# Two decode layers on one core: a 22nd cache unit kept on chip between the layers, four slots left for what is loaded there

## The chip, the cores and the metric

The kernel runs on one core of a Trainium2 chip. The metric is device time in microseconds (us), the median of three runs; lower is better. Beside it stands one profiled execution, whose trace gives the durations used below.

## The reference

The same pair of blocks is applied twice to a row `x` of 448 numbers for each of 2 batch entries (B = 2, D = 448): an attention block over a cache, and a gated feed-forward block (called FFN below). All data is float32.

```python
def _A_ref(x, k_cache, v_cache, wq, wo):        # H = 16 heads, Dh = 256, Sk = 4096
    q = (x @ wq) ... one query of 256 per head and batch entry
    scores = einsum("bhqd,bhkd->bhqk", q, k_cache) * Dh ** -0.5
    p = softmax(scores)
    o = einsum("bhqk,bhkd->bhqd", p, v_cache)
    return o ... @ wo
def _B_ref(x, W_gate, W_up, W_down):             # F = 1792
    gate = relu(x @ W_gate); up = x @ W_up
    return (gate * up) @ W_down

x = x + _A_ref(_layernorm(x), k_cache, v_cache, wq, wo)
x = x + _B_ref(_layernorm(x), W_gate, W_up, W_down)
x = x + _A_ref(_layernorm(x), k_cache, v_cache, wq, wo)      # same weights, same cache
x = x + _B_ref(_layernorm(x), W_gate, W_up, W_down)
```

The cache has 32 pairs of a head and a batch entry. Keys and values of one pair are 4 MB each, so one attention block reads 256 MB and the whole kernel a little over twice that.

## The kernel before

**Slots and units.** All loaded data goes through one on-chip tile, `arena`, cut into 27 slots of 128 partitions by 2048 numbers (1 MB): 24 slots in three blocks of eight, and three single slots. A quarter of one pair's keys or values fills one slot and is called a unit here: `("k", pair, c)` or `("v", pair, c)` with c from 0 to 3. The weights of one head (query and output projection, `("h", head, 0)`), one of seven parts of `W_gate` and `W_up` (`("in", "", c)`, here in 0 to in 6) and one of four parts of `W_down` (`("out", "", c)`, here out 0 to out 3) also take one slot each, with 128x1792 numbers or less (896 KB). Units go into the 24 block slots alone, a head's weights into the three single slots alone, and FFN weights into a single slot first and otherwise into any.

**The list of loads.** `pending` is a list of all loads in a fixed order: those of the first attention (pass 1), the eleven FFN loads, those of the second attention (pass 2), the eleven FFN loads again. `pump()` (L115) takes loads from its front as long as a slot of the right kind is free and issues each as a DMA from SyncE (SP in the profile); when the first in the list finds no slot, nothing behind it goes. It is called whenever `release()` (L144) frees a slot, that is, behind the last instruction that reads the slot. So each DMA waits on SP for the reader whose release made it possible, and the DMAs keep the order of the list.

**What is kept over the turn.** The turn is the end of pass 1, the FFN, and the start of pass 2. Pass 2 goes through the pairs in the order `second`, which begins with the last four pairs of pass 1. Units in the set `keep` (L186) are not released by pass 1, stay in their slots over the FFN, and are left out of the loads of pass 2. Before the change `keep` has the weights of the first head, the first 20 units of pass 2 (keys of pairs 0, 1 and 2, values of pairs 0 and 1, four each) and the last quarter of the values of pair 2: 21 units and one head, 22 slots. Five slots are left for the FFN's eleven loads, two of them single slots. As `keep` takes the loads for granted, pass 2 loads first, in this order: three quarters of the keys of pair 3, the weights of two heads (`heads`, placed by L192), the last quarter of those keys, three quarters of the values of pair 2, and then whole sets of four.

**The work at the turn.** The FFN (`ffn`, L560) first makes the layer's input row ready (`absorb`), then multiplies it with in 0 to in 3 (L576, 32 matmuls), with in 3 again and in 4 (16 matmuls), in 5 (8) and in 6 (8), with other matmuls of TensorE (PE) in between, then with out 0 to out 3 (L669). Each part is released behind its last matmul. Pass 2 starts with the scores of pair 0 on VectorE and ScalarE (`score`, L393 on): a kept unit is released behind its score. The query of pair 2 (`query`, L326) is made in the first iteration of pass 2, between scores, and needs the first of the two heads.

**In the steady part** of a pass, `score_block` (L370) works on the keys of one pair with two long VectorE instructions (L378 and L386), and `weigh` (L453) multiplies the values on TensorE. Several megabytes of loads are in the DMA queue at any time there.

Of the kernel before, what the change touches and what calls it, by code (L numbers as in the profile page):

```python
# [21 lines left out]
NC = NT // CT  # L22
# [48 lines left out]
def two_layers(  # L71
# [77 lines left out]
    second = first[-1:-5:-1] + first[:-4]  # L149
    behind = dict(zip(first[1:], first))  # L150

    def loads(order, whole, cuts):


        found = [(("h", order[0][0], 0), 1)]

        def some(kind, u):
            c = 0
            for n in cuts.get((kind, u), (NC,)):
                found.append(((kind, order[u], c), n))  # L160
                c += n

        for u, unit in enumerate(order):
            if u in whole:
                found.append((("k", unit, 0), PAIR))
            else:
                some("k", u)
                if u > 0:
                    some("v", u - 1)
            if u % 2 and u + 1 < len(order):  # L170
                found.append((("h", order[u + 1][0], 0), 1))
        some("v", len(order) - 1)
        return found
# [10 lines left out]
    of_second = loads(second, WHOLE_SECOND, early | at_end)  # L184

    keep = {of_second[0][0], *[key for key, _ in of_second if key[0] != "h"][:KEPT]}  # L186
    keep.add(("v", second[2], NC - 1))
    of_second = [(key, n) for key, n in of_second if key not in keep]

    heads = [(key, n) for key, n in of_second if key[0] == "h"][:2]  # L190
    of_second = [part for part in of_second if part not in heads]
    of_second[NC - 1 : NC - 1] = heads  # L192
    pending += of_first + [(key, 1) for key in ffn_loads]
    pending += of_second + [(key, 1) for key in ffn_loads]

# [617 lines left out]
def build(nc, shapes):  # L813
    import concourse.tile as _tile

    args = [
        nc.dram_tensor(f"in_{n}_dram", s, F32, kind="ExternalInput").ap() for n, s in shapes.items()
    ]
    for i, (shape, _) in enumerate(_OUTS):
        args.append(nc.dram_tensor(f"out_{i}_dram", shape, F32, kind="ExternalOutput").ap())  # L820
    with _tile.TileContext(nc) as tc:
        two_layers(tc, *args)
# [12 lines left out]
```

## Time and profile before

| | before |
|---|---|
| median of 3 runs | 1320.49 us (1320.46 to 1320.8) |
| the profiled execution's own time | 1320.27 us |
| its span, first to last instruction | 1318.5 us |
| moved by DMA in the span | 563.16 MB, mean 427 GB/s |
| busy: VectorE / TensorE / GpSimd / ScalarE | 82% / 42% / 20% / 15% |
| granted TensorE clock, mean | 0.682 |

The time outside the span is 1.8 us. All times in the trace are counted from the start of the span. In the tables of stretches that the prediction shows, "DMA share" is the mean busy share of the core's 16 DMA engines; a little over 1.00 stands for full, since packets of one engine overlap slightly in the records. A line of the DMA issues gives size and the time from issue to landing, where the profile can tell it.

### The profile page before, as it was taken

The page shows a single profiled execution, that of the slowest core. Times are in us where ns is not written, and L with a number is a line of the kernel's source. Part 1 is how long each engine was busy: PE and PEld are TensorE (multiplying, and loading weights), DVE is VectorE, ACT ScalarE, POOL GpSimd, SP SyncE. Part 2 cuts the span into 40 slices and gives each one's busy share as a digit, 9 for nine tenths or more (in the row PEclk, how much of TensorE's full clock was granted, in tenths as well). Part 3 has the DMA queues.
Part 4 walks back from the last instruction along what each step waited for, and adds up shares of the span by engine and source line. Part 5 has one row for each costly group of instructions (what it writes and reads, how often), then busy time and mean ns, then how long its engine had stood idle before and what let it go on. Part 6 is the DMA issues. An engine that isn't in the chain of part 4 may idle for free.

```text
span 1318.5 us, 9085 instructions
## 1 busy us (share of the span) xinstructions
PE 553.7 (42%) x3276; PEld 190.6 (14%) x3276; DVE 1081.6 (82%) x780; ACT 195.6 (15%) x776; POOL 269.0 (20%) x192
## 2 busy tenths in 40 slices
PE   2243342433434324345585444242433424434348
PEld 2011010110111101112141111110111101101113
DVE  4989888898888988888729987798888988877892
ACT  2100000000000000212026513000000000012241
POOL 0002003322133220321001153030123331230210
PEclk9675666656667667666697777666767667666679
DMA  9999999999999999999999999999999999999998
GB/s 408 435 430 429 432 428 437 432 436 434 417 445 435 430 430 426 445 418 430 421 405 416 431 430 435 438 432 430 432 431 436 433 428 436 429 432 425 427 425 334
DMA packets 22665, 563.16 MB, mean 427 GB/s; under 512 B 2520, under 2 KB 2652, under 8 KB 9564
## 3 DMA queue, kind: packets, MB, share of 16 engines
q1 hardware_dynamic: 22612, 562.57, 99.5%
q8 instruction: 26, 0.43, 0.1%
q14 instruction: 19, 0.16, 0.0%
q10 hardware_dynamic: 8, 0.00, 0.0%
HBM read 562.56 MB, written 0.00 MB: 427 GB/s over the span
## 4 chain that ended last, share of the span: by engine, by line
DMA 55%; DVE 32%; PE 7%; POOL 2%; issue 2%; ACT 1%; DVEq 0%; SPq 0%; POOLq 0%; ACTq 0%
DMA arena<-in_vk_dram 54%; DVE arena L378 12%; DVE scores L386 11%; DVE arena L409 3%; DVE down L418 2%; PE po L462 2%; POOL top L429 2%; DVE arena L418 2%; DMA arena<-in_w_out_dram 1%; DVE row L478 1%; PE small L488 1%; PE acc L511 1%; DVE scores L415 1%; ACT arena L411 1%; PE pf L576 1%
## 5 line engine op out<-in xcount | busy, mean ns | idle before, releaser
L378 DVE TENSOR_TENSOR arena<-arena 128x8192 f32<-128x8192 f32 x51 | 443.3, 8692 | 111.0 <-DMA arena<-in_vk_dram 110.9
L386 DVE TENSOR_REDUCE scores<-arena 128x32 f32<-128x8192 f32 (+1 forms) x53 | 431.8, 8148 | 0.0
L488 PE MATMUL small<-ones,row 128*128 128x1 f32 x256 | 62.0, 346 | 686.3 <-DVE row L478 686.3
L462 PE MATMUL po<-arena,probs 128*2 128x512 f32 x2048 | 303.1, 734 | 10.3 <-DMA arena<-in_vk_dram 6.6
L429 POOL PARTITION_ALL_REDUCE top<-mx x64 | 64.6, 1009 | 645.8 <-DVE mx L427 645.8
L443 POOL PARTITION_ALL_REDUCE total<-rs x64 | 176.1, 2752 | 61.3 <-ACT probs L437 60.3
L488 PEld LDWEIGHTS small<-ones,row 128*128 128x128 f32 x256 | 56.5, 308 | 748.9 <-DVE row L478 748.9
L434 ACT ACTIVATE nm<-top,nsr 128x1 f32<-128x1 f32 x64 | 18.8, 294 | 612.4 <-POOL top L429 612.4
L354 POOL PARTITION_BROADCAST arena<-arena x58 | 27.6, 545 | 300.6 <-ACT arena L350 300.6
L462 PEld LDWEIGHTS po<-arena,probs 128*2 128x2 f32 x2048 | 54.8, 96 | 198.3 <-issue 191.2
L338 PE MATMUL pq<-arena,xs 128*33 128x256 f32 x174 | 70.6, 571 | 14.1 <-DMA arena<-in_w_head_dram 14.1
L511 PE MATMUL acc<-arena,oT 128*2 128x448 f32 x128 | 50.9, 894 | 32.1 <-DVE oT L501 32.1
L350 ACT ACTIVATE arena<-pq 33x256 f32<-33x256 f32 x29 | 10.9, 377 | 321.7 <-PE pq L342 321.7
L382 ACT ACTIVATE arena<-arena 128x256 f32<-128x256 f32 x104 | 41.7, 402 | 86.2 <-DVE arena L378 86.2
L478 DVE SCALAR_TENSOR_TENSOR row<-po,lead,row 128x256 f32<-128x256 f32 x64 | 30.7, 479 | 25.8 <-ACT row L475 25.4
L411 ACT ACTIVATE arena<-arena 128x256 f32<-128x256 f32 x117 | 47.1, 404 | 20.4 <-DVE arena L409 20.1
L409 DVE TENSOR_TENSOR arena<-arena 128x1024 f32<-128x1024 f32 (+1 forms) x24 | 42.0, 1748 | 0.0
L338 PEld LDWEIGHTS pq<-arena,xs 128*33 128x33 f32 x174 | 25.3, 162 | 81.3 <-issue 66.7
L475 ACT ACTIVATE row<-po,lead 128x256 f32<-128x256 f32 x64 | 29.1, 455 | 21.2 <-PE po L462 21.2
L418 DVE SCALAR_TENSOR_TENSOR down<-arena,pq 128x256 f32<-128x256 f32 x64 | 26.9, 420 | 5.4 <-DMA arena<-in_vk_dram 3.4
L501 DVE TENSOR_TENSOR oT<-small,ri 128x4 f32<-128x4 f32 x32 | 5.1, 161 | 29.0 <-PE small L488 29.0
L437 ACT ACTIVATE probs<-scores,nm,sr 128x32 f32<-128x32 f32 x64 | 26.4, 413 | 2.1
(145 smaller groups left out, 359.0 us busy)
## 6 DMA issues: line engine op xcount, KB each, us to landing
arena<-in_vk_dram SPq DMA_DIRECT2D x16, 4096.0 KB, 40.0
arena<-in_w_head_dram SPq DMA_DIRECT2D x31, 896.0 KB, 30.9
arena<-in_vk_dram SPq DMA_DIRECT2D x27, 1024.0 KB, 14.9
arena<-in_vk_dram SPq DMA_DIRECT2D x12, 2048.0 KB, 38.5
arena<-in_w_in_dram SPq DMA_DIRECT2D x14, 896.0 KB, 26.2
arena<-in_w_out_dram SPq DMA_DIRECT2D x5, 896.0 KB, 8.9
arena<-in_vk_dram SPq DMA_DIRECT2D x47, 43.4
arena<-in_w_out_dram SPq DMA_DIRECT2D x1, 512.0 KB, 17.3
```

Of the source, the lines that this page charges most:

```text
L338: nc.tensor.matmul(q, xs[:, c, :], w[:, c * DH : (c + 1) * DH], start=(c == 0), stop=False)
L378: nc.vector.tensor_mul(kt, kt, q_of[u][:, None, :].to_broadcast([P, NT, DH]))
L386: nc.vector.reduce_sum(s_of[u][:, shared:], kt[:, shared:, :], axis=AX.X)
L409: nc.vector.tensor_mul(some, some, q_of[u][:, None, :].to_broadcast([P, whole, DH]))
L411: nc.scalar.activation(kt[:, t, :], kt[:, t, :], AF.Copy, accum_out=found[:, t : t + 1])
L418: nc.vector.scalar_tensor_tensor(junk if kept else kt[:, t, :], kt[:, t, :], 1.0, q_of[u], op0=ALU.mult, op1=ALU.mult, accum_out=found[:, ...
L429: nc.gpsimd.partition_all_reduce(mx_of[u], mx, P, RED.max)
L443: nc.gpsimd.partition_all_reduce(total[:, b : b + 1], rs, P, RED.add)
L462: nc.tensor.matmul(po_of[u][32 * t : 32 * t + 2, :], p_of[u][:, n : n + 2], vt[:, 2 * t * DH : (2 * t + 2) * DH], start=(c == 0), stop=(c ...
L478: nc.vector.scalar_tensor_tensor(row[:, :DH], po_of.pop(u)[:, DH:], lead[:, 1:2], row[:, :DH], op0=ALU.mult, op1=ALU.add,)
L488: nc.tensor.matmul(pT_of[u - u % 2][:, c, b : b + 1], row[:, c * P : (c + 1) * P], ones, start=True, stop=True,)
L511: nc.tensor.matmul(acc[at : at + B], oT_of[h][:, c, :], wo[:, c * D : (c + 1) * D], start=(n < 3), stop=(n >= n_u - 3),)
```

## The change

One more unit is kept: the third quarter of the values of pair 2 in the order of pass 2 stays in its slot, beside the fourth. With 22 units and one head, 23 of the 27 slots are taken over the FFN and four are free, two of them single. One load of 1 MB leaves the list of pass 2. In that list the weights of the two heads now come first, ahead of all keys of pair 3, where three units stood ahead of them before.

```diff
     keep = {of_second[0][0], *[key for key, _ in of_second if key[0] != "h"][:KEPT]}
-    keep.add(("v", second[2], NC - 1))
+    keep |= {("v", second[2], c) for c in (NC - 2, NC - 1)}
     of_second = [(key, n) for key, n in of_second if key not in keep]
 
     heads = [(key, n) for key, n in of_second if key[0] == "h"][:2]
     of_second = [part for part in of_second if part not in heads]
-    of_second[NC - 1 : NC - 1] = heads
+    of_second[:0] = heads
```

The instructions of TensorE, VectorE, ScalarE and GpSimd stand in the same order as before. On SP one DMA is gone and two have moved. The first piece below is SP's queue between the FFN of the turn and the start of pass 2, with - for before and + for after (`in_vk_dram` holds keys and values, 128x2048 is one unit, `in_w_head_dram` the weights of a head, `in_w_out_dram` those of `W_down`):

```order
 L131 DMA arena<-in_w_out_dram 128x1792 x3
 L131 DMA arena<-in_w_out_dram 128x896
-L131 DMA arena<-in_vk_dram 128x2048 x3
 L131 DMA arena<-in_w_head_dram 128x1792 x2
-L131 DMA arena<-in_vk_dram 128x2048 x20
+L131 DMA arena<-in_vk_dram 128x2048 x22
 L131 DMA arena<-in_w_head_dram 128x1792
 L131 DMA arena<-in_vk_dram 128x8192 x4
```

The two heads have moved ahead of three units, and 23 single units have become 22; everything behind is as it was. What this piece does not show is for which reader each DMA waits. The second piece is SP's queue over the FFN's own loads, with the engines and queues that each waits for (PE is TensorE; the DMAHW names are earlier DMAs):

```order
 L131 DMA arena<-in_w_in_dram 128x1792 [waits DMAHW3_49,PE_49]
 L131 DMA arena<-in_w_in_dram 128x1792 [waits DMAHW4_49,PE_49]
-L131 DMA arena<-in_w_in_dram 128x1792 [waits DMAHW5_49,PE_49]
-L131 DMA arena<-in_w_in_dram 128x1792 [waits DVE_49,DMAHW6_49,PE_49,Pool_49]
-L131 DMA arena<-in_w_in_dram 128x1792 [waits DMAHW7_49,DMAHW2_49,PE_49]
-L131 DMA arena<-in_w_in_dram 128x1792 [waits DMAHW3_49,DMAHW0_49,PE_49]
-L131 DMA arena<-in_w_out_dram 128x1792 [waits DMAHW4_49,DMAHW1_49,PE_49]
-L131 DMA arena<-in_w_out_dram 128x1792 [waits DMAHW5_49,PE_49]
+L131 DMA arena<-in_w_in_dram 128x1792 [waits DVE_49,DMAHW5_49,PE_49,Pool_49]
+L131 DMA arena<-in_w_in_dram 128x1792 [waits DMAHW6_49,DMAHW2_49,PE_49]
+L131 DMA arena<-in_w_in_dram 128x1792 [waits DMAHW7_49,DMAHW3_49,PE_49]
+L131 DMA arena<-in_w_in_dram 128x1792 [waits DMAHW4_49,DMAHW0_49,PE_49]
```

The wait that also names DVE and Pool is for the slot of a head of pass 1, which is released late in that pass. Before, in 4 took it; now in 3 takes it, and in 4 is the first load that waits for a matmul of the FFN itself (on in 0, whose slot it takes). Each load from in 4 on now waits for the release that the load behind it waited for before.

## The prediction

> **What bounds the kernel now.** I read the head of the page first, then who waits for whom, then the turn in stretches.
>
> ```profile
> DMA packets 22665, 563.16 MB, mean 427 GB/s; under 512 B 2520, under 2 KB 2652, under 8 KB 9564
> q1 hardware_dynamic: 22612, 562.57, 99.5%
> DVE arena L378 <- DMA arena<-in_vk_dram: 110.9, 47, 13.1
> ```
>
> SP's queue keeps the 16 DMA engines busy for 99.5% of the span, and VectorE, the busiest compute engine, waits 111 us in 47 pieces for keys to land. The bound is the DMA engines. So I ask two things of the change: how many bytes less, and how much longer the engines stand dry. The next rows are stretches of the turn (share of the DMA engines and GB/s at the end of each row).
>
> ```profile
> 660.00:668.00 8.00, 7.50 (x47) 2.67 (x40) 1.34 (x6) 2.36 (x4) 0.00 (x0) 1.00 1.01 419
> 668.00:669.00 1.00, 0.91 (x12) 0.40 (x14) 0.81 (x6) 0.02 (x1) 0.00 (x0) 1.00 0.83 344
> 669.00:670.00 1.00, 1.00 (x19) 0.37 (x12) 0.13 (x1) 0.00 (x0) 0.00 (x0) 1.00 0.65 272
> 670.00:671.00 1.00, 1.00 (x16) 0.25 (x12) 0.00 (x0) 0.00 (x0) 0.00 (x0) 1.00 0.73 201
> 671.00:673.00 2.00, 2.00 (x16) 0.67 (x17) 0.00 (x0) 0.05 (x1) 0.00 (x0) 1.00 0.96 387
> 673.00:690.00 17.00, 14.97 (x187) 8.74 (x179) 4.32 (x21) 4.16 (x19) 0.00 (x0) 1.00 1.02 420
> 690.00:702.00 12.00, 6.57 (x30) 4.32 (x34) 11.86 (x55) 8.70 (x38) 1.68 (x4) 0.85 1.02 414
> ```
>
> The engines are full before 668 and after 673. Between, they are short by 0.17 + 0.35 + 0.27 + 2 x 0.04 = 0.87 us. This one dry place of before lies exactly where the change takes a slot away. SP's issues there, and under them the time to landing of the first, second and last:
>
> ```profile
> 632.09 0.33 SPq L131 DMA_DIRECT2D arena<-in_w_in_dram  x1
> 647.38 0.33 SPq L131 DMA_DIRECT2D arena<-in_w_in_dram  x1
> 669.46 0.33 SPq L131 DMA_DIRECT2D arena<-in_w_in_dram  x1
> 670.96 0.33 SPq L131 DMA_DIRECT2D arena<-in_w_out_dram  x1
> ...
> arena<-in_w_in_dram SPq DMA_DIRECT2D x1, 896.0 KB, 32.1
> arena<-in_w_in_dram SPq DMA_DIRECT2D x1, 896.0 KB, 23.4
> arena<-in_w_out_dram SPq DMA_DIRECT2D x1, 896.0 KB, 8.5
> ```
>
> These are in 0, in 3, in 5 and out 0. In 0 lands at 632.09 + 32.1 = 664.2, in 3 at 670.8, so one load of 896 KB takes 2.2 us and in 4, queued behind in 3, lands at about 673.0. In 5 had to wait for the release of in 0 and came at 669.46. At 668.1 the first engines had no work left, in 4 done, while the slowest was still at in 3 (landing 670.8): the 16 engines are not in step, and run out over 668.1 to 673.0, a spread of 4.9 us.
>
> **The change part by part.** *One load of 1 MB less.* 1,048,576 bytes at the 420 GB/s of the stretch after the dip are 2.5 us of all 16 engines. That is the whole gain, and 0.19% of the time; about 0.2% (2.6 us) is what a measurement of this kernel can tell from no change.
>
> *In 4 behind the wait.* With four free slots, in 4 takes the slot of in 0 and is issued at 669.46, where in 5 was. In 5, in 6 and out 0 each move one release later too, but lie behind in 4 in a queue that is not empty. The engines now run out behind in 3, 2.2 us earlier: over 665.9 to 670.8. The new load reaches them at about 670.9, in the middle of the stretches in which the share climbs from 0.73 to 0.96. If they run out evenly, the mean dry time of before is (670.9 - 668.1)^2 / (2 x 4.9) = 0.80 us, near the 0.87 read from the rows, so the picture holds; of after it is (5.0 + 0.1) / 2 = 2.55 us. That is 1.7 us more for the mean engine. Bounds: an engine that ran dry before 670.9 already loses the full 2.2 more; the slowest, still busy with in 3 until 670.8, about 0.1.
>
> So an engine gains between 2.5 - 2.2 = 0.3 and 2.5 - 0.1 = 2.4 us, 0.8 in the mean. The time is set by the engine that is last at the end:
>
> ```profile
> 1306.00:1310.00 4.00, 3.89 (x29) 1.21 (x24) 0.62 (x1) 0.00 (x0) 0.00 (x0) 1.00 1.01 410
> 1310.00:1313.00 3.00, 2.75 (x66) 1.91 (x64) 1.06 (x6) 0.71 (x3) 0.00 (x0) 1.00 0.61 241
> 1313.00:1318.00 5.00, 2.67 (x68) 1.72 (x62) 0.79 (x2) 0.78 (x3) 0.00 (x0) 1.00 0.07 24
> ```
>
> The engines finish over about 4 us again, 640 us behind a restart that had brought most of them into step. As much spread grows in pass 2 alone as in pass 1, so I take it as made anew, the last engine at the end being any of them, and the gain as the mean one, 0.8.
>
> *TensorE waits for weights.* Before, its matmuls on the FFN weights ran without a gap:
>
> ```profile
> 668.45 3.40 PE L576 MATMUL pf<-arena,xs 128*32 128x448 f32 x32
> 672.84 1.71 PE L576 MATMUL pf<-arena,xs 128*32 128x448 f32 x16
> 675.54 0.96 PE L576 MATMUL pf<-arena,xs 128*32 128x448 f32 x8
> 677.50 0.96 PE L576 MATMUL pf<-arena,xs 128*32 128x448 f32 x8
> ...
> arena<-in_w_head_dram SPq DMA_DIRECT2D x1, 896.0 KB, 4.7
> ```
>
> In 4 is needed in the middle of the second row, at 673.7, in 5 at 675.54, in 6 at 677.50. The last row is the kernel's first load, with nothing ahead of it: 4.7 us. By that, in 4 lands at 674.2, in 5 at 676.4 and in 6 at 678.6: 0.5, 0.9 and 1.1 us too late, and the FFN ends 1.1 us later. The other bound is in 4 at 673.0, as before, with nobody waiting.
>
> The Trainium skill's page "DMA: Bandwidth & Descriptors", section "Anatomy of one DMA", gives a transfer about 2.0 us fixed plus its bytes at 436 GB/s, fitted on the GpSimd path. By that estimate 896 KB land after 4.1 us, in 4 at 673.6, the FFN would end 0.5 us later, and the sum below would be 0.8 instead of 0.6. The trace's first load took 4.7, so the sum goes by 4.7.
>
> *The start of pass 2.* A later FFN releases the next slots later, and one slot fewer is queued. Issues of pass 2's first releases, and time to landing of the first three:
>
> ```profile
> 691.46 0.33 SPq L131 DMA_DIRECT2D arena<-in_vk_dram  x1
> 694.67 0.33 SPq L131 DMA_DIRECT2D arena<-in_vk_dram  x1
> 699.56 0.33 SPq L131 DMA_DIRECT2D arena<-in_vk_dram  x1
> 702.79 0.33 SPq L131 DMA_DIRECT2D arena<-in_vk_dram  x1
> ...
> arena<-in_vk_dram SPq DMA_DIRECT2D x1, 1024.0 KB, 8.8
> arena<-in_vk_dram SPq DMA_DIRECT2D x1, 1024.0 KB, 8.0
> arena<-in_vk_dram SPq DMA_DIRECT2D x1, 1024.0 KB, 8.1
> arena<-in_vk_dram SPq DMA_DIRECT2D x8, 1024.0 KB, 20.5
> ```
>
> A unit with nothing ahead would take 4.7 + 0.3 = 5.0 us; the rest is cover: 3.8, 3.0 and 3.1 us. The one issued at 702.79 lands 2.5 us behind the one before it, at 710.2, so its cover is 2.4, the thinnest. After the change one unit less is ahead (-2.5), the release comes 1.1 later (-1.1), and the queue itself runs 1.2 later since in 4 lands at 674.2 and not 673.0 (+1.2). At 702.79 that leaves 0.0, elsewhere 0.6 or more. The cover is used up and just not broken; engines ahead of the others run out there for a moment. I take 0.2 us, with bounds 0 and, if the queue is not later while the releases are, 1.2. Further on (last row: eight issues from 714 to 729) the cover is 15 us and nothing reaches the DMA engines.
>
> *Heads first.* Three units and two heads exchange places, the same bytes. The two slots freed by out 0 and out 1 are the single ones, so the heads go at once; a unit standing first would have had to wait for out 2.
>
> ```profile
> PE pq L338 <- DMA arena<-in_w_head_dram: 0.5, 1, 0.5
> ```
>
> The 0.5 us that TensorE waited for the first head goes, which saves nothing, since no load waits for that query. The three units land some 5.6 us later (2 x 2.2 for the heads, 1.2 for in 4); they belong to pair 3, and at 702.79 VectorE had only released the first unit of pair 1. SP has one instruction of 0.33 us less and is no bound. Both cost nothing.
>
> **Sum.** -2.5 + 1.7 + 0.2 = -0.6 us. The profiled execution's 1320.27 becomes 1319.7; it lies 0.22 below the median of 1320.49, so the forecast for the median is **1319.9 us**.
>
> **The rivals.** *The whole load is gained.* If the engine that is last at the turn is also last at the end, by nature and not by chance, it never stood dry and gains 2.4: 1318.1 us. For it: two spreads of the same size. Against: the restart took its lag away, and it would have kept a lead in lateness over the others at the end.
>
> *A second dry place, on the other side: slower.* If in 6 comes over 1.1 us late, or the queue does not run later with it, the issue at 702.79 finds the engines empty. An ordinary engine gains only 0.3 at the turn and loses 1.2 here: +0.9, 1321.4 us. It decides from a cover below -0.3 us on.
>
> *TensorE's clock falls.* The three new waits stand in a stretch at full clock, and elsewhere a thinly used TensorE runs at half:
>
> ```profile
> 610.00:620.00 10.00, 4.76 (x13) 2.73 (x14) 8.43 (x40) 0.36 (x2) 0.35 (x1) 0.50 1.02 437
> ```
>
> From 673 to 690 TensorE is busy for 14.97 us; at half the clock that chain would take between 0 and 15 us more, say 8, every release of pass 2 come 8 us later against covers of 2.4 to 3.8, and the engines stand dry for some 6: 1326 us. Against it: 0.5, 0.4 and 0.2 us are short beside the 5.2 us that TensorE rested in that row. The Trainium skill's page "TensorE: Matmul & The Clock Gate", section "Part 1: The HAM clock gate", has the clock halved after an idle window of about 3.4 us, which speaks against this rival too; no run here shows that length.
>
> **How the numbers follow.** The forecast, 1319.2 to 1320.7 by its own terms (0.3 to 1.3 gained at the turn, 0 to 0.5 lost behind it), gets 0.58; the whole load gained 0.20; the second dry place 0.13; the clock 0.04; a gain beyond the load 0.03; another loss 0.02. The range reaches from the whole gain to the second dry place, 1318.0 to 1321.5, and leaves out about 0.1. Over 0.2% faster is under 1317.9, past the whole load: 0.04 with the edge of the second case. Over 0.2% slower is above 1323.1: the clock, other losses, 0.06. The rest, 0.90, lies within.
>
> **What would show it.** The steps are right if the changed profile shows: 562.1 MB; in 4 issued near 669.5; the DMA share between 665 and 671 short by about 2.5 us instead of 0.87; TensorE waiting for in 4, in 5 and in 6 by 0.5 us or less each; DMA share at 1.0 again from 673 on, 702 included. The forecast is wrong if the share dips a second time around 700 to 706, if TensorE's clock in the FFN is under 1.00, or if the last engines end a whole 2.4 us earlier.

## The result, and the profile after

The changed kernel takes 1322.77 us, the kernel before 1320.73 us beside it (medians of 22 runs each): a ratio of 1.0017, 95% interval 1.0011 to 1.0022. It is slower by 2.0 us, where a gain of 0.6 us was forecast, and lies outside the range that was given (1318.0 to 1321.5), though within 0.2% of the time before. The runs also spread more: 1321.4 to 1324.98, against 1320.33 to 1321.58.

The bytes went as announced. From the page of the changed kernel:

```profile
span 1321.2 us, 9079 instructions
DMA packets 22521, 562.11 MB, mean 425 GB/s; under 512 B 2504, under 2 KB 2636, under 8 KB 9548
```

1 MB less is moved, and the span is 2.7 us longer; so the DMA engines lost some 5 us more than before. Where, the stretches of the changed kernel's turn show (share of the DMA engines and GB/s at the end of each row):

```profile
660.00:668.00 8.00, 6.87 (x39) 1.96 (x37) 0.76 (x3) 1.67 (x4) 0.00 (x0) 1.00 0.96 398
668.00:671.00 3.00, 2.91 (x31) 1.52 (x34) 1.52 (x10) 0.71 (x1) 0.00 (x0) 1.00 0.23 96
671.00:673.00 2.00, 2.00 (x18) 0.36 (x10) 0.00 (x0) 0.00 (x0) 0.00 (x0) 1.00 0.86 287
673.00:685.00 12.00, 8.68 (x82) 4.04 (x81) 1.84 (x6) 1.98 (x7) 0.00 (x0) 1.00 1.01 418
685.00:693.00 8.00, 7.30 (x110) 5.04 (x109) 2.72 (x15) 2.48 (x13) 0.00 (x0) 1.00 0.98 353
693.00:698.00 5.00, 3.99 (x22) 2.91 (x22) 5.00 (x23) 4.28 (x17) 0.00 (x0) 1.00 1.01 419
698.00:706.00 8.00, 1.89 (x13) 0.40 (x16) 7.86 (x33) 4.96 (x24) 1.71 (x4) 0.68 0.98 332
706.00:714.00 8.00, 3.54 (x28) 0.49 (x17) 7.59 (x29) 5.12 (x24) 0.58 (x1) 0.89 1.01 388
```

Where before had one dip, there are three: behind in 3 (660 to 673), behind out 3 (685 to 693) and at the start of pass 2 (698 to 714). In these long rows two of them hardly show in the share, 0.98 and more; GB/s tells them, 353 and 332 against 420. Rows of one microsecond show how the first dip comes about, the engines running out one behind the other, and that the share does fall inside the third:

```profile
668.00:669.00 1.00, 1.00 (x11) 0.71 (x10) 0.81 (x6) 0.71 (x1) 0.00 (x0) 1.00 0.45 186
669.00:670.00 1.00, 0.91 (x13) 0.46 (x16) 0.72 (x6) 0.00 (x0) 0.00 (x0) 1.00 0.19 79
670.00:671.00 1.00, 1.00 (x16) 0.35 (x11) 0.00 (x0) 0.00 (x0) 0.00 (x0) 1.00 0.05 22
702.00:703.00 1.00, 0.00 (x0) 0.00 (x0) 0.90 (x6) 0.10 (x2) 0.08 (x1) 0.50 0.64 197
```

Below, "dry time" is read from GB/s: the length of a stretch times (1 - GB/s / 420). The two kernels in the same stretches, the kernel before first (674 to 684, not shown, is full in both, at 423 and 420 GB/s):

```profile
660.00:674.00 14.00, 13.41 (x98) 4.62 (x92) 2.94 (x16) 3.08 (x6) 0.00 (x0) 1.00 0.94 383
684.00:697.00 13.00, 10.75 (x98) 7.53 (x98) 9.26 (x47) 7.38 (x31) 0.00 (x0) 0.87 1.02 419
697.00:716.00 19.00, 8.39 (x49) 2.48 (x51) 18.41 (x69) 13.23 (x61) 3.38 (x6) 0.72 1.01 412
```

The changed kernel:

```profile
660.00:674.00 14.00, 12.78 (x92) 4.30 (x90) 2.38 (x13) 2.78 (x6) 0.00 (x0) 1.00 0.79 317
684.00:697.00 13.00, 10.83 (x134) 7.66 (x129) 6.72 (x34) 6.40 (x28) 0.00 (x0) 1.00 0.99 379
697.00:716.00 19.00, 6.43 (x40) 1.45 (x37) 18.36 (x73) 12.06 (x56) 3.33 (x6) 0.78 0.99 369
```

That is 1.2, 0.0 and 0.4 us of dry time before, and 3.4, 1.3 and 2.3 us after: 1.6 against 7.0.

What TensorE met in the FFN of the changed kernel (its rows in order of time, with the idle time before each and what ended it), and two issues of SP with the landing of the second:

```profile
669.13 3.37 PE L576 MATMUL pf<-arena,xs 128*32 128x448 f32 x32
673.50 0.96 PE L576 MATMUL pf<-arena,xs 128*32 128x448 f32 x8
674.77 0.96 PE L576 MATMUL pf<-arena,xs 128*32 128x448 f32 x8 [0.31 <-DMA arena<-in_w_in_dram]
678.05 0.96 PE L576 MATMUL pf<-arena,xs 128*32 128x448 f32 x8 [1.26 <-DMA arena<-in_w_in_dram]
680.24 0.96 PE L576 MATMUL pf<-arena,xs 128*32 128x448 f32 x8 [0.16 <-DMA arena<-in_w_in_dram]
```

```profile
670.14 0.33 SPq L131 DMA_DIRECT2D arena<-in_w_in_dram  x1
670.90 0.33 SPq L131 DMA_DIRECT2D arena<-in_w_in_dram  x1
...
arena<-in_w_in_dram SPq DMA_DIRECT2D x1, 896.0 KB, 7.1
```

In 4 is issued at 670.14, behind the release of in 0, and its matmuls start as it lands, at 674.77: 4.6 us. In 5 takes 7.1 us, about a microsecond more than one load behind in 4 should. The three waits come to 1.73 us. From the first matmul on in 0 (669.13) to the first on out 0 (683.24) the FFN takes 14.1 us, where it took 12.0 before (668.45 to 680.48): 2.1 us longer. It also starts 0.7 us later, and in 0 was issued 0.5 us later already (632.60 against 632.09). So part of the 2.8 us between the two profiled executions (1323.08 and 1320.27) lies ahead of the FFN and is not the change's.

The first loads that pass 2's releases bring in the changed kernel, and the landings of the first four:

```profile
694.23 0.33 SPq L131 DMA_DIRECT2D arena<-in_vk_dram  x1
697.43 0.33 SPq L131 DMA_DIRECT2D arena<-in_vk_dram  x1
699.42 0.33 SPq L131 DMA_DIRECT2D arena<-in_vk_dram  x1
702.53 0.33 SPq L131 DMA_DIRECT2D arena<-in_vk_dram  x1
705.76 0.33 SPq L131 DMA_DIRECT2D arena<-in_vk_dram  x1
...
arena<-in_vk_dram SPq DMA_DIRECT2D x1, 1024.0 KB, 7.2
arena<-in_vk_dram SPq DMA_DIRECT2D x1, 1024.0 KB, 6.7
arena<-in_vk_dram SPq DMA_DIRECT2D x1, 1024.0 KB, 7.6
arena<-in_vk_dram SPq DMA_DIRECT2D x1, 1024.0 KB, 6.9
```

Before, the first, second, fourth and fifth of these five were issued at 691.46, 694.67, 699.56 and 702.79, so they now come 2.8 to 3.0 us later. As before they come about 2.8 us apart, more than the 2.5 us that a unit takes the engines, and the first four land 6.7 to 7.6 us after their issue although the engines run dry around them.

### The profile page after: what moved, and what is told of

Same layout as the page of the kernel before. It is cut to its first block, busy times and chain, and to the rows that moved or that the text cites. A ratio compares the mean times of both kernels' runs of the same rounds, so it can differ in the third digit from the quotient of the medians.

```text
span 1321.2 us, 9079 instructions
## 1 busy us (share of the span) xinstructions
PE 565.6 (43%) x3276; PEld 191.9 (15%) x3276; DVE 1081.7 (82%) x780; ACT 195.7 (15%) x776; POOL 268.3 (20%) x192
## 4 chain that ended last, share of the span: by engine, by line
DMA 63%; DVE 25%; PE 8%; issue 1%; POOL 1%; ACT 1%; DVEq 0%; SPq 0%; POOLq 0%; ACTq 0%
DMA arena<-in_vk_dram 60%; DVE arena L378 12%; DVE scores L386 8%; PE po L462 2%; DMA arena<-in_w_in_dram 2%; DVE arena L409 2%; DVE arena L418 2%; PE pq L338 1%; DMA arena<-in_w_out_dram 1%; PE acc L511 1%; POOL top L429 1%; DVE down L418 1%; PE small L488 1%; DVE row L478 1%; ACT arena L411 1%
## 5 line engine op out<-in xcount | busy, mean ns | idle before, releaser
L338 PE MATMUL pq<-arena,xs 128*33 128x256 f32 x174 | 77.1, 613 | 11.8 <-DMA arena<-in_w_head_dram 11.8
```

What stands on the lines that cost most here:

```text
L338: nc.tensor.matmul(q, xs[:, c, :], w[:, c * DH : (c + 1) * DH], start=(c == 0), stop=False)
```

## The experiments

Times are medians beside the kernel before on the same chip (1320.66 to 1320.70 us in the three groups). The stretch 660 to 740 holds the whole turn. Its last number, GB/s, is compared over all kernels in the table at the end; it is 412 in the kernel before and 384 in the changed one:

```profile
660.00:740.00 80.00, 56.23 (x427) 23.72 (x423) 53.05 (x208) 40.75 (x175) 7.66 (x12) 0.85 1.00 412
```

```profile
660.00:740.00 80.00, 52.36 (x411) 20.90 (x409) 50.36 (x200) 37.94 (x163) 7.18 (x11) 0.89 0.97 384
```

### The two parts of the change alone

The new order alone, on the kernel before:

```diff
-    of_second[NC - 1 : NC - 1] = heads
+    of_second[:0] = heads
```

> 21 units kept as before, but the two heads first: the new order alone. Theory A (slots: what counts is when a load finds a slot of its kind): with five free slots the two single ones come free with out 2 and out 3, so the heads at the front hold up the three units that could have gone with in 6, out 0 and out 1 (issued at 678.5, 681.6 and 683.4 before). Five loads then start at about 685 to 687, the engines have run out behind out 3, dry for some 3 us more than before: about 1323.7 us, a dip in GB/s at 683 to 687. Theory B (the order of heads and units does not matter, the extra unit alone does): the same as before, 1320.7 us.

Measured: 1324.54 us (ratio 1.0029, 1.0018 to 1.0039). Its stretch 684 to 688:

```profile
684.00:688.00 4.00, 4.00 (x71) 2.90 (x70) 0.66 (x4) 0.82 (x6) 0.00 (x0) 1.00 0.36 97
```

The kept unit alone, on the kernel before:

```diff
-    keep.add(("v", second[2], NC - 1))
+    keep |= {("v", second[2], c) for c in (NC - 2, NC - 1)}
```

> 22 units kept, heads behind three units as before: the kept unit alone. Theory A: with four free slots the slots of out 0 and out 1 are the single ones, so the first unit waits until out 2 is released, 3.7 us later than the first head goes in the changed kernel: dry at the end of the FFN for some 3 us more than the changed kernel, about 1326 us. Theory B (the extra unit alone costs the 2 us): as the changed kernel, 1322.8 us.

Measured: 1325.68 us (1.0036, 1.0024 to 1.0049); its stretch 684 to 688:

```profile
684.00:688.00 4.00, 3.53 (x67) 2.74 (x64) 0.38 (x2) 0.87 (x5) 0.00 (x0) 1.00 0.44 178
```

Both as theory A had it: each part alone is worse than the two together, by 1.8 and 2.9 us. The order belongs to the number of slots, since it decides whether the first load in the list finds a slot of its kind. With the kept unit, heads first is the right order; the loss is not the order's.

### One slot more

20 units kept, heads first:

```diff
-    keep.add(("v", second[2], NC - 1))
...
-    of_second[NC - 1 : NC - 1] = heads
+    of_second[:0] = heads
```

> 20 units kept, six free slots, heads first, which suits the slots that come free there: the step to the other side. Theory A (a closed loop of free slots, dry where their number is too small): one load of 1 MB more costs 2.5 us, the 1.2 us that the engines of before are dry at the turn go: about 1322.0 us (+1.3), no dip in GB/s between 664 and 672. Theory C (the free slots do not limit the DMA engines, something else in the changed kernel does): the full 2.5 us more, 1323.2 us.

Measured: 1323.18 us (1.0018, 1.001 to 1.0027), 2.5 us over the kernel before.

```profile
660.00:740.00 80.00, 56.44 (x428) 23.66 (x430) 52.95 (x208) 40.86 (x175) 7.61 (x12) 0.85 1.01 419
```

The row shows that the engines are never dry, and the time rises by the whole load nevertheless. Theory A fell in its number: the 1.2 us that the kernel before is dry behind in 4 cost it nothing. So dry time is not simply paid.

### Halves

The changed kernel with 22 loads of the turn issued as two DMAs each:

```diff
+    loaded = []
...
             parts = [0, src.shape[1]]
+            if turn + 0 <= len(loaded) < turn + 22:
+                parts[1:1] = [src.shape[1] // 2]
+            loaded.append(1)
...
+    turn = len(of_first)
```

> The changed kernel, with each of the 22 loads from in 0 on to the last of the first nine units of pass 2 issued as two DMAs of half its columns. A half can start when its half of the slot has been read, and its readers can start when it has landed. Theory A (loop time of a slot): every slot comes round 1 to 1.5 us sooner, the three dry stretches shrink by about half of the 5.3 us that they hold beyond those of before: about 1320.3 us, 2.5 less than the changed kernel. Theory D (each DMA into an empty queue pays a start of its own, and more DMAs pay it more often): no gain or a loss, 1322.8 to 1324 us.

Measured: 1322.93 us (1.0016, 1.0007 to 1.0025), no gain; theory D's number, though its reason, that each start costs, is not shown by it. Its stretches from 660 show that the stretch from 684 to 697 gained 0.8 us (404 GB/s against 379), the full one before it lost 0.5 (398 against 420), and the two large ones hardly moved:

```profile
660.00:674.00 14.00, 12.82 (x92) 4.61 (x86) 2.65 (x15) 3.08 (x6) 0.00 (x0) 1.00 0.81 314
674.00:684.00 10.00, 8.22 (x73) 3.66 (x67) 1.47 (x4) 0.91 (x3) 0.00 (x0) 1.00 1.02 398
684.00:697.00 13.00, 10.83 (x130) 7.74 (x129) 6.99 (x34) 6.68 (x29) 0.00 (x0) 1.00 1.03 404
697.00:716.00 19.00, 6.11 (x38) 1.31 (x36) 18.37 (x73) 12.06 (x57) 3.40 (x6) 0.77 1.01 371
```

### Readers made faster

The changed kernel with less VectorE work on pair 0 in pass 2:

```diff
+                wide = DH // 4 if ahead and u == 0 else DH
                 for t in range(whole, CT):
                     nc.vector.scalar_tensor_tensor(
-                        junk if kept else kt[:, t, :], kt[:, t, :], 1.0, q_of[u],
+                        junk[:, :wide] if kept else kt[:, t, :wide], kt[:, t, :wide], 1.0,
+                        q_of[u][:, :wide],
...
```

> The changed kernel, with the VectorE products of pair 0 in pass 2 taken over 64 of 256 numbers only (three quarters of these are left out), so that its kept slots come free about 1 us sooner each. Theory E (the DMA engines may stand dry for about 2.3 us in the mean at the turn at no cost, since they are out of step by that; every further dry microsecond is paid): the third dry stretch, 697 to 716, goes with its 2.3 us, of 7.1 us dry 4.8 remain, 2.5 of them paid: about 1320.6 us. Theory F (the third stretch only follows from the late FFN and is caught up later): as the changed kernel, 1322.8 us.

Measured: 1321.34 us (1.0005, 0.9997 to 1.0014). The stretch 697 to 716 rose from 369 to 394 GB/s, from 2.3 to 1.2 us dry:

```profile
697.00:716.00 19.00, 7.07 (x52) 2.91 (x55) 14.79 (x55) 13.15 (x62) 3.38 (x6) 0.86 1.00 394
```

It lies between the two numbers: the third stretch is half gone, not whole, and 1.4 us came back. Theory F, by which it is caught up later, is out.

The changed kernel with the FFN's start freed from the attention's end:

```diff
-        absorb(acc[:SUMS], SUMS, lead, nlead)
+        if last:
+            absorb(acc[:SUMS], SUMS, lead, nlead)
+        else:
+            nc.scalar.activation(row[:SUMS, :D], acc[:SUMS], AF.Copy)
```

> The changed kernel, with the FFN of the turn not waiting for the attention's result (the update of its input row, VectorE and TensorE work of some 2.4 us, is left out), so that in 0 is released some 2.4 us sooner. Theory E: the first stretch loses 2.2 to 2.4 us of its 3.4, the two behind it most of their 3.7; dry time 1 to 2.5 us, none or 0.2 of it paid, and 22 units give their whole 2.5 us: 1318.1 to 1318.6 us. Theory F (the fourth slot itself, with the starts of single loads in an empty queue, is what costs): at most the first stretch gains, 1320.5 to 1322 us.

Measured: 1321.18 us (1.0005, 0.9996 to 1.0014).

```profile
660.00:674.00 14.00, 11.69 (x82) 3.25 (x86) 1.26 (x7) 2.99 (x5) 0.00 (x0) 1.00 0.89 355
684.00:697.00 13.00, 11.30 (x102) 7.47 (x99) 8.49 (x42) 7.72 (x33) 0.00 (x0) 0.87 0.99 380
```

Theory E's number was missed by nearly 3 us; the time lies in theory F's range. The first stretch lost 1.2 of its 3.4 us, the second nothing (380 GB/s against 379), the third 1.0 of its 2.3 (392 against 369). The FFN's first matmul came at 667.12, 2.0 us sooner, but then TensorE waited 1.3 us for in 3: four slots do not come round fast enough even when the FFN starts sooner.

Both at once, and both with the loads from out 0 on in halves (the diff of the halves with `turn + 7`):

> The changed kernel with both leavings-out: the FFN of the turn does not wait for the attention's result, and three quarters of VectorE's products of pair 0 in pass 2 are left out. Dry time by the two single experiments: 5.1 - 1.1 = 4.0 us. Theory E: 1.6 us of it are paid, 1319.8 us, faster than the kernel before (1320.7) by 0.9, so that 22 units pay as soon as the slots come round fast enough. Theory H (22 units never pay, four slots being too few whatever the readers do): 1321 us or more.

Measured: 1320.83 us (1.0001, 0.9992 to 1.001).

> The same, and the loads from out 0 to the ninth unit of pass 2 issued as two halves each, which in the kernel with halves took 0.8 us from the second dry stretch (the halves of the first FFN loads, which cost 0.5 us between 674 and 684, are left whole here). Theory E: dry time about 3.2 us, 0.8 paid: 1319.0 us. Theory D (more DMAs cost as much as they bring): as the run with both leavings-out, 1319.8 us.

Measured: 1320.43 us (0.9999, 0.999 to 1.0007).

The two rows, in this order:

```profile
660.00:740.00 80.00, 55.50 (x406) 22.07 (x409) 46.20 (x196) 39.77 (x170) 7.60 (x12) 0.84 0.99 398
```

```profile
660.00:740.00 80.00, 55.30 (x416) 21.56 (x418) 48.03 (x204) 41.38 (x178) 7.67 (x12) 0.85 0.99 396
```

The gains that were expected did not come, and the two cannot be told apart. With some of the work around the turn left out, 22 units draw level with 21; ahead they are not. Neither theory's number is confirmed, for the first or for the second, and what a fully sufficient speed-up would give was not reached.

### Slower readers and fewer slots

The kernel with 20 units and six free slots, with two and with four filling matmuls ahead of the FFN's:

```diff
         busy(2)
+        for _ in range(2 if not last else 0):
+            busy(8)
         total = squares()
```

> The kernel with 20 kept units and six free slots, which shows no dry stretch, with two idle-filling matmuls of about 1 us each ahead of the FFN's matmuls at the turn: every release of the turn comes some 2 us later. Theory E (up to about 2.3 us of dry time are free): dry time 1 to 2 us, the time stays at 1323.2 us (within 0.3). Theory G (dry time is paid from the first microsecond): 1324.2 to 1325.2 us.

Measured: 1323.45 us (1.0021, 1.0012 to 1.003), 0.3 over the same kernel without them.

```profile
660.00:740.00 80.00, 54.18 (x415) 21.71 (x413) 51.26 (x203) 38.88 (x166) 7.62 (x12) 0.87 1.00 409
```

> The same with four filling matmuls, some 4 us later. Theory E: dry time 3.5 to 5.5 us, of which all but 2.3 is paid: 1324.4 to 1326.4 us, and in any case the dry time read from the trace less 2.3. Theory G: 1326.7 to 1328.7 us, the whole dry time.

Measured: 1325.28 us (1.0034, 1.0021 to 1.0046).

```profile
660.00:740.00 80.00, 59.43 (x428) 23.27 (x420) 49.04 (x193) 37.32 (x159) 6.80 (x11) 0.83 0.97 395
```

The FFN's first matmul starts 1.4 and 4.1 us later than without the fillers, and dry time is 2.1 and 4.8 us by these rows. The first costs 0.3, the second 2.1: both theory E's, and theory G, by which every dry microsecond is paid, is out.

23 units, three free slots:

```diff
-    keep |= {("v", second[2], c) for c in (NC - 2, NC - 1)}
+    keep |= {("v", second[2], c) for c in (NC - 3, NC - 2, NC - 1)}
```

> 23 units kept, three slots free, heads first: one step further in the direction of the change. Theory E (the dry time less 2.4 us is paid, against 2.5 us for each unit kept): the dry time grows by more than the 2.5 us that the unit gives, to 12 us or more; about 1326 us, and in any case 1315.7 plus the dry time of the trace less 2.4. Theory F2 (the loss of the change comes from its one bad meeting of in 4 with the empty queue, and a further unit gains): at most 1322.8 us.

Measured: 1327.29 us (1.0054, 1.0041 to 1.0067).

```profile
660.00:740.00 80.00, 56.00 (x383) 24.01 (x377) 45.59 (x183) 35.25 (x150) 5.09 (x8) 0.77 0.87 338
```

The next step in the same direction loses 4.5 us more, as theory E had it in sign and nearly in size. The profiled execution was the slowest of its five, 3.3 us over their median.

### All of them together

"Paid" is the profiled execution's own time over a line of 1320.5 us less 2.5 us for each kept unit over 21, the price of 1 MB at 420 GB/s (20 units without a dry stretch measure 2.52 over the kernel before).

| kernel | units | GB/s, 660 to 740 | dry, us | profiled time | paid, us | dry in the last 20 us of the span |
|---|---|---|---|---|---|---|
| 20, heads first | 20 | 419 | 0.2 | 1322.86 | -0.1 | 8.2 |
| before | 21 | 412 | 1.5 | 1320.27 | -0.2 | 6.7 |
| 20, two fillers | 20 | 409 | 2.1 | 1323.64 | 0.6 | 6.9 |
| both leavings-out | 22 | 398 | 4.2 | 1321.20 | 3.2 | 6.8 |
| the same, halves | 22 | 396 | 4.6 | 1321.00 | 3.0 | 6.9 |
| FFN not waiting | 22 | 395 | 4.8 | 1320.35 | 2.4 | 6.0 |
| 20, four fillers | 20 | 395 | 4.8 | 1325.76 | 2.8 | 6.6 |
| order alone | 21 | 389 | 5.9 | 1324.23 | 3.7 | 6.3 |
| fewer scores | 22 | 388 | 6.1 | 1322.05 | 4.1 | 6.5 |
| halves | 22 | 385 | 6.7 | 1322.58 | 4.6 | 6.3 |
| the change | 22 | 384 | 6.9 | 1323.08 | 5.1 | 6.1 |
| kept unit alone | 22 | 370 | 9.5 | 1326.27 | 8.3 | 7.1 |
| 23 units | 23 | 338 | 15.6 | 1330.60 | 15.1 | 8.0 |

Whatever made the engines dry, and at whichever of the three places, what is paid is the dry time less some 2 us (0.5 to 2.4 in the eleven rows with more than 2 us). With the medians in place of the profiled times it is 1.4 to 2.8 us, and 3.8 for 23 units.

The last column shows where these 2 us go. It is dry time in the same sense at the end of the kernel, where the engines run out. Three of its rows, for 20 units with heads first, the kernel before and the changed kernel:

```profile
1301.10:1321.10 20.00, 16.71 (x221) 8.24 (x217) 5.31 (x24) 4.11 (x11) 0.00 (x0) 1.00 0.61 247
1298.50:1318.50 20.00, 16.55 (x217) 8.18 (x217) 5.30 (x24) 3.57 (x11) 0.00 (x0) 1.00 0.69 279
1301.20:1321.20 20.00, 16.51 (x218) 8.24 (x217) 5.31 (x24) 3.79 (x11) 0.00 (x0) 1.00 0.72 292
```

The kernel that is never dry at the turn is dry for longest at the end. Dry time at the turn and at the end together, less what is paid, is 8.3 to 8.6 us in eleven of the thirteen rows, and 7.8 and 7.9 in the two others. So the first 2 us at the turn look free because the engines would otherwise have stood dry for about as long at the end. With 15.6 us at the turn the end is hardly shorter, and nearly all of it is paid.

## Why the prediction was wrong, step by step

*The bound and the gain* were right: the engines are the bound, and 1 MB is worth 2.5 us, no more and no less (20 units against 21).

*In 4 behind the wait* was right in place and nearly in size: in 4 came behind the release of in 0 and the first stretch grew by 2.2 us of dry time, 1.7 forecast.

*TensorE waits* were right in kind. In 4 landed after 4.6 us, near the first load's 4.7. The 4.1 us worked out from the Trainium skill's page "DMA: Bandwidth & Descriptors", section "Anatomy of one DMA", was short. In 5 came a microsecond later than one load behind it, so the sum was 1.73 and not 1.1 us, and the FFN took 2.1 us longer.

*The start of pass 2* is the step that failed. The term was put at 0.2 us, at most 1.2; the trace has 1.9 us more dry time from 697 to 716 than before. Two sizes in it were wrong. The cover was taken as landing time less 5.0 us, a figure made from the kernel's first load, and came out as 2.4 to 3.8 us. The loads that in the changed kernel met a queue that ran dry took 6.7 to 7.6 us. By 7.1, the middle of these, the cover before was 0.3 to 1.7 us, less than the 2.5 us of the slot that went. And the releases, forecast 1.1 us later, came 2.8 to 3.0 us later, 2.1 of it from the longer FFN. No run separates the two. The releases there, 2.8 us apart, are slower than the engines, so the shortage stays until pair 1, when two come together.

*A place was left out.* The two heads and the first units of pass 2, behind the releases of out 0 to out 3, were taken to have cover without a row being read for it. They did not: 1.3 us dry from 684 to 697.

With the sizes of the trace the prediction's own sum is -2.5 + 2.2 + 1.3 + 1.9 = +2.9 us, beside +2.8 between the two profiled executions and +2.0 between the medians.

*The mean engine* was the wrong measure as well, though it is not what turned the sign. The prediction took the spread at the end as made anew in pass 2, whatever happened at the turn, and so the mean dry time as paid. By that the 1.2 us that the kernel before is dry would be paid; the kernel with six free slots has none of them and gains nothing, since it is dry for 1.5 us more at the end. Had the first stretch been the only one, its 3.4 us would have cost some 1.4 by this estimate, and the unit would have gained a microsecond; no run has that stretch alone.

*The rivals.* The one that ended on the other side, the second dry place, was the right mechanism at too small a price (two places and 3.2 us, not one and 1.2), and had 0.13. Its condition, in 6 over 1.1 us late, was met: its matmuls start at 680.24, 2.7 us later than before. The whole load gained, with 0.20, had a sound reason for the first stretch alone: the share is still 0.05 from 670 to 671, which is about one engine in sixteen, and back at 0.77 in the next microsecond, so the last engine hardly stood dry there. The two later stretches undid it. TensorE's clock stayed at 1.00 from 660 to 698, so that rival was rightly small. Of the signs that had been named, the second dip of the share between 700 and 706 did come: 0.64 with 197 GB/s from 702 to 703. A reader of longer rows would have missed it, since the row from 698 to 706 has 0.98 beside 332 GB/s.

That the engines are out of step explains why dry time moves from the end to the turn: those that run out early at the turn would have run out early at the end. This is argued from the falling share in the rows from 668 to 671 and the sums of the table; the packets in the trace do not name their engine, so it is not shown engine by engine. Why in 5 took a microsecond more also stays open.

## What to carry to other kernels

Where a few slots go round between loads and readers, price a slot by the loop it makes: what counts is whether (slots x transfer time) covers landing, reading and release, at every place of the stretch and not only at the first wait. In the changed kernel the slot of out 0 is loaded at 674.52 and again at 684.35: 9.8 us, and four transfers of 2.2 us are 8.8. Before, it was 670.96 to 681.58, 10.6 us, and five transfers are 11.0. Size the cover of a queue by loads that met it nearly empty in the same stretch, not by a lone load at the start, and read dry stretches from GB/s, since the busy share of a long row can stay near 1. Look at the end of the kernel too before you price a dry stretch. The kernel before stands just where the dry time is still free: a unit fewer costs its whole 2.5 us, and a unit more costs about twice what it saves.

## What the runs showed of the hardware

The DMA engines' busy share was 0.98 to 1.01 in stretches of 8 us that moved 332 to 388 GB/s, and 1.01 at 418 to 420: a share near 1 does not show that the engines move bytes at their full rate. The 16 engines run out one behind the other: behind in 3 the share fell over 668 to 671 from 0.45 to 0.05. Dry time of up to about 2 us at the turn cost nothing in the total, whichever kernel had it, and the end was shorter for it: 8.2 us dry in the last 20 without a dry turn, 6.0 to 7.1 in the kernels with 1.5 to 9.5 us at the turn, and 8.0 again in the one with 15.6. And a load into a queue running dry lands after 4.6 to 7.6 us, with a spread that a single figure does not hold.
